# Parallel attention plus product-key experts on one Trainium2 core: two activation blocks moved ahead of the one-hot rows, the last gate stores moved behind loads, attention added into resident totals

## The chip, the core and the metric

The kernel runs on one core of one Trainium2 chip. The metric is device time in microseconds (us) of one execution; three runs of the kernel before are known, and one profiled execution with its trace. In the profile PE is TensorE (PEld its weight loads), DVE is VectorE, ACT is ScalarE, POOL is GpSimd, SP is SyncE, whose queue issues nearly all DMAs. Rows give start and length in us, or a group's busy us and the mean ns of one instruction.

## What is computed

All in float32: 2048 tokens of width 512, 32 heads of width 16, one key and one value head. The second branch has 32 product-key heads, each of which picks 2 of 4096 experts.

```python
x = A_x
xn = _layernorm(x, axis=-1)
return x + _A_ref(xn, A_wq, A_wk, A_wv, A_wo) + _B_ref(xn, B_w_q, B_k1, B_k2, B_u, B_v)

# A: p = softmax(q k^T * Dh**-0.5); out = (p v) @ wo
# B, per token and head: s1, s2 = 64 scores against k1 and k2; the best two of each,
#    the best two of their four sums (top_s, top_e)
g = _softmax(top_s, axis=-1)
ue = u[top_e]; ve = v[top_e]
act = _gelu(jnp.einsum("nd,nhkd->nhk", xf, ue))
out = jnp.einsum("nhk,nhk,nhkd->nd", g, act, ve)
```

## The kernel before

The 2048 tokens are 16 tiles of 128, in four groups of four tiles. Attention needs an exponential for every score, 1024 calls of 128x1024 on ACT, and runs through the whole kernel as 256 steps (`att_steps`, L1040): four pairs of score matmuls (`sc`), four exponentials, sixteen probability-value matmuls (`pv`). Everything else is laid into these steps by hand; no engine's order is left to a scheduler in the main loop (L1147), and every engine runs its queue strictly in the order written.

**The experts** have two ways. Tokens of groups 0 and 1 gather their rows of `u` and `v` by indirect DMA (`gather`, L876); a row is a *slot*: a dot with the token (`dot`, L888), later an add of the weighted row into the tile's total (`add`, L921), both on DVE. Groups 2 and 3 are *dense phases* (`dense`, L648): all 4096 experts are multiplied, in 32 blocks of 128. For a block, 12 matmuls of 128x512 (each product in three split terms, since float32 operands are split into a rounded high half and a rest) give the activations of 512 tokens (`pact`, L799); gelu and the gate rows make `wd`, again as halves; and for each pair of blocks 24 matmuls (`pout`, L783) add into the four totals. The gates of a dense phase come from *one-hot rows*: 32 groups of 16 tokens; for each, DVE compares two index rows with a row of numbers (`onehot`, L721) and 16 small matmuls (`pg`, L752) spread the gates to experts x tokens. ACT copies them to `gst` tiles, which SP stores to `d_g` in DRAM in packets of 256 bytes, two stores of 16 blocks each for every 64 tokens (L760). Each block then reads its 128x512 gate rows back (`fetch_gates`, L669). The `gst` tiles and the `wd` tiles share four buffers; the gate tiles `gy` have three.

**Ahead of a dense phase** the scores of its tokens are made in eight columns c of four tiles each (`item`, L513): 12 matmuls, then 8 maxima and 8 index searches on DVE; after the fourth tile `batch` (L564) makes indices and, through a list that is run two steps later, an exponential and the gates. Then `dense` starts: GpSimd copies the numbers to `io` (L704), the first weights are asked for (`fetch`, L654), three groups of transposes (`ptd`, L714) turn indices and gates into rows.

**What sets the order.** Each step has a `mid` (ACT's and DVE's lists) and a `fill`, in which the score thread (a Python generator) is run until its count of PE time, `spent`, reaches `aim`; at most 4.0 a step are taken. What it yields is a cost; a yield of None ends the step's fill. `store` puts a DMA on a list that SP gets at the start of the next step; `on_act` and `behind` put work on ACT's and DVE's lists of the next `mid`; LAST and LATER hold work for one and two steps on. `dense_on` picks the rate of slots: 1.7 a step outside a phase, 2.5 in its blocks, 1.4 in its one-hot rows; from step 192 of 256 on the rest is spread evenly (L1154).

**The two branches meet** tile by tile. Attention's output for a tile (`block_out`, L423) is either kept: copied to the one `fin` buffer by ACT and stored in `d_part` (L440), to be loaded and added when the experts' total is done (`experts_out`, L446, L452); or, where the experts came first, the stored total is loaded into `fin` and attention's part added to it (L433). Tiles 8 to 11 take the second way, in four steps at the end of the second dense phase's one-hot rows; tiles 0 to 7 the first.

Of the kernel before, what the change touches and what calls it, by code (L numbers as in the profile page):

```python
# [23 lines left out]
P = 128  # L24
# [30 lines left out]
def tile_kernel(ctx, tc, x, wq, wkv, wo, wqT, kT, uv, ub, vb, out):  # L55
# [17 lines left out]
    d_w = [dram.tile([P, KC, 2, 512], F32, name=f"dw{c}") for c in range(NC)]  # L73
    d_g = dram.tile([NB, P, 512], F32, name="dg")
# [164 lines left out]
    def zero_m():  # L239
        z = gtile()  # L240
        nc.gpsimd.memset(z, 0.0)
        nc.sync.dma_start(d_m.rearrange("a h s -> (a h s)").rearrange("(p n) -> p n", p=P), z)

# [140 lines left out]
    DONE_A, DONE_B, OUTS = {}, {}, []  # L384
    WO, lent = [], [0]
# [37 lines left out]
    def block_out(qb, j):  # L423
# [5 lines left out]
        if t in FIN:  # L429
# [14 lines left out]
        DONE_A[t] = True  # L444

    def experts_out(t):  # L446
# [3 lines left out]
        if t in FIN:  # L450
            fin = FIN.pop(t)
            nc.vector.tensor_add(fin, fin, ACC[t])  # L452
            store(lambda: nc.sync.dma_start(out[t * P:(t + 1) * P, :], fin))
        elif t in DONE_A:
# [5 lines left out]
        DONE_B[t] = True  # L460
        return True
# [94 lines left out]
    DT = []  # L556
# [7 lines left out]
    def batch(ph, c, b):  # L564
# [52 lines left out]
        if c == 0:  # L617
            DT.clear()
            dense_tiles()
# [14 lines left out]
        def gates():  # L634
# [8 lines left out]
            stt(dgt[:, :, 1, w], gg, GS, gh, op0=OP.mult, op1=OP.subtract)  # L643

# [3 lines left out]
    def dense(DG, after):  # L648

        df1, df2, dgt = DT[:3]  # L650
# [12 lines left out]
        def gate_tile(b):  # L663
            if b not in gates:
                gy = late[0].tile([P, 2, 512], F32, name="gy", tag="gy", bufs=3)
                gates[b] = gy
            return gates[b]

        def fetch_gates(b):  # L669
            if b < NB and b not in fetched:  # L670
                if formed[0] < b - 2:
# [3 lines left out]
                nc.sync.dma_start(gate_tile(b)[:, 0, :], d_g[b])  # L675
                fetched.add(b)

        splits, halved = {}, set()

        def split(b):  # L680
            if b < NB:
                if b not in raws:
                    run(STORES)
                rw = raws.pop(b)
                us, vs = wk_tile(), wk_tile()
                for i, w in enumerate((us, vs)):
                    nc.scalar.copy(w[:, 0, :], rw[:, i, :])  # L687
                    behind(lambda w=w, i=i: nc.vector.tensor_tensor(out=w[:, 1, :], in0=rw[:, i, :], in1=w[:, 0, :],  # L688
                                                                    op=OP.subtract))
                behind(lambda: halved.add(b))  # L690
                splits[b] = us, vs
# [11 lines left out]
        io = kt(F16, (P, P, TB))  # L703
        nc.gpsimd.tensor_copy(io, iota_h[:, :, None].to_broadcast([P, P, TB]))  # L704
        fetch(0)
        fetch(1)
        yield None
        tr = kt(F16, (P, 3, 512))
        for n, src in enumerate((df1, df2, dgt)):
            if n == 2:  # L710
                yield None
# [550 lines left out]
```

## Time and profile before

| What | Value |
|---|---|
| Runs (device time) | 1992.71, 2001.25, 2004.34 us; median 2001.25 |
| Profiled execution, device time | 2001.03 us |
| Its span, first to last instruction | 1999.3 us |
| Mean granted TensorE clock | 0.967 |
| First dense phase: transposes, one-hot matmuls, blocks | from 607.7, from 618.0, from 753.5 us |
| Second dense phase: the same | from 1451.0, from 1460.4, from 1570.9 us |
| DMA | 494.79 MB, mean 247 GB/s |

A span is a little shorter than the execution's time. The busy shares of all engines are means over stages with different limits, so a stretch is read by itself: in the view by windows each row is a stretch with the busy time and count of each engine, the granted clock of TensorE in it and the share of the DMA engines. In the timeline a bracket tells how long the engine was idle before the group and what released it. The chain of waits follows the work that ended last back from the end. A DMA's row in SP's queue is its issue; in the chain it is issue to landing.

### The profile page before, as it was taken

The numbers are of one execution on the slowest core, as the hardware profiler recorded it, in microseconds if no ns is written. First come the engines' busy times: TensorE is split into PE (matmuls) and PEld (weight loads), VectorE is DVE, ScalarE is ACT, GpSimd is POOL, SyncE is SP. The second block draws the span as 40 slices with busy tenths as digits, with TensorE's granted clock in tenths as the row PEclk, the third lists the DMA queues.
The fourth block names the chain that finished last, engine by engine and source line by source line (L and its number), as shares of the span: only waits on it lengthen the run. The fifth ranks groups of instructions, "written<-read, shape, count | busy, mean of one in ns | idle before, by whom it ended". The sixth has DMA issues, their size and how long they took to land.

```text
span 1999.3 us, 34729 instructions
## 1 busy us (share of the span) xinstructions
PE 1882.9 (94%) x10990; PEld 997.5 (50%) x10990; DVE 1682.7 (84%) x6713; ACT 1292.0 (65%) x1804; POOL 570.8 (29%) x542
## 2 busy tenths in 40 slices
PE   6869999999998998999999999999899789999997
PEld 4534444555554444555555455555445345555552
DVE  7537888999998786999999779999999668999993
ACT  3236666655556785787877565555568567788873
POOL 2202232222222232333444222222223333333320
PEclk9989999999997998999999999999979899999999
DMA  7847878977664878888889877777568877888762
GB/s 272 301 185 235 276 272 272 331 275 248 218 212 140 229 221 271 264 269 269 284 297 328 286 253 261 268 238 225 176 169 234 276 245 263 268 277 257 263 211 63
DMA packets 239882, 494.79 MB, mean 247 GB/s; under 512 B 93380, under 2 KB 93380, under 8 KB 239692
## 3 DMA queue, kind: packets, MB, share of 16 engines
q0 software_dynamic: 73728, 268.47, 40.5%
q1 hardware_dynamic: 163960, 222.44, 34.0%
q10 hardware_dynamic: 2004, 1.61, 0.3%
q8 instruction: 88, 1.44, 0.3%
q14 instruction: 102, 0.84, 0.1%
HBM read 429.51 MB, written 57.64 MB: 244 GB/s over the span
## 4 chain that ended last, share of the span: by engine, by line
PE 63%; DVE 20%; DMA 5%; issue 2%; ACT 2%; SPq 1%; DVEq 0%; ACTq 0%
PE pv L332 18%; PE sc L318 12%; PE psc L532 10%; PE pout L783 8%; PE pact L799 8%; DVE i L547 5%; DVE xa L930 4%; DVE m L545 3%; DVE g L895 3%; PE pg L752 3%; PE pw L487 2%; PE pwo L427 1%; DMA dg<-gst 1%; ACT pt L321 1%; DMA fin<-dpart 1%
## 5 line engine op out<-in xcount | busy, mean ns | idle before, releaser
L321 ACT ACTIVATE pt<-sc 128x1024 f32<-128x1024 f32 x1024 | 993.0, 1025 | 471.1 <-PE sc L318 424.6
L883 POOL DMA_INDIRECT g<-in_uv_dram,idx x512 | 554.0, 1082 | 1358.4 <-DVE xa L930 697.4
L332 PE MATMUL pv<-pt,vaug 128*32 128x512 f32 x4096 | 524.1, 631 | 0.0
L318 PE MATMUL sc<-qa,kaug 64*128 64x512 f32 x2048 | 389.1, 454 | 14.4 <-ACT pt L321 13.5
L532 PE MATMUL psc<-wk,xt 128*128 128x512 f32 x1536 | 388.2, 400 | 5.3 <-DMA xt<-dxt 3.2
L930 DVE SCALAR_TENSOR_TENSOR xa<-g,w,xa 128x512 f32<-128x512 f32 x512 | 370.6, 745 | 0.0
L895 DVE CUSTOM_DVE_ANT_0 g<-g,xa 128x512 f32<-128x512 f32 x512 | 336.1, 681 | 3.0 <-DMA g<-in_uv_dram,idx 3.0
L532 PEld LDWEIGHTS psc<-wk,xt 128*128 128x128 f32 x1536 | 277.8, 188 | 108.7 <-issue 38.5
L318 PEld LDWEIGHTS sc<-qa,kaug 64*128 64x128 f32 x2048 | 157.6, 187 | 338.2 <-ACT pt L321 203.5
L332 PEld LDWEIGHTS pv<-pt,vaug 128*32 128x32 f32 x4096 | 110.7, 113 | 263.4 <-issue 261.7
L799 PE MATMUL pact<-xt,wk 128*128 128x512 f32 x768 | 198.7, 404 | 14.6 <-DVE fin L433 6.3
L547 DVE FIND_INDEX8 i<-m,psc 128x8 uint32<-128x64 f32 x1024 | 206.4, 221 | 0.0
L783 PE MATMUL pout<-wk,wd 128*128 128x512 f32 x768 | 195.7, 402 | 8.7 <-DVE wd L835 4.7
L799 PEld LDWEIGHTS pact<-xt,wk 128*128 128x128 f32 x768 | 141.1, 190 | 65.4 <-issue 17.7
L783 PEld LDWEIGHTS pout<-wk,wd 128*128 128x128 f32 x768 | 140.6, 188 | 56.7 <-DVE wd L835 6.0
L545 DVE MAX8 m<-psc 128x8 f32<-128x64 f32 x1024 | 146.0, 214 | 22.2 <-PE psc L532 19.8
L786 DVE TENSOR_TENSOR da<-da,pout 128x512 f32<-128x512 f32 x128 | 82.7, 679 | 8.2 <-PE pout L783 7.9
L918 DVE SCALAR_TENSOR_TENSOR w<-gth,ga 128x4 f32<-128x4 f32 x128 | 20.2, 158 | 79.9 <-ACT gth L911 79.4
L688 DVE TENSOR_TENSOR wk<-rw,wk 128x512 fp32r<-128x512 f32 x128 | 84.8, 682 | 0.1
L725 DVE TENSOR_TENSOR oh<-oh 128x2048 f16<-128x2048 f16 x64 | 78.0, 1219 | 7.1 <-PE pg L752 7.1
L752 PE MATMUL pg<-oh 128*128 128x32 f16 x1024 | 73.4, 246 | 8.1 <-DVE oh L728 8.1
L687 ACT CAST wk<-rw 128x512 fp32r<-128x512 f32 x128 | 73.6, 628 | 9.0 <-DMA rw<-in_ub_dram 6.7
(150 smaller groups left out, 1341.8 us busy)
## 6 DMA issues: line engine op xcount, KB each, us to landing
wk<-dw SPq DMA_DIRECT2D x96, 512.0 KB
wqt<-in_wqT_dram SPq DMA_DIRECT2D x32, 512.0 KB
dw<-wk SPq DMA_DIRECT2D x32, 512.0 KB
rw<-in_ub_dram SPq DMA_DIRECT2D x64, 256.0 KB
rw<-in_vb_dram SPq DMA_DIRECT2D x64, 256.0 KB
dg<-gst SPq DMA_DIRECT2D x32, 512.0 KB
gy<-dg SPq DMA_DIRECT2D x64, 256.0 KB
qa<-dqh SPq DMA_DIRECT2D x128, 64.0 KB
```

Of the source, the lines that this page charges most:

```text
L318: nc.tensor.matmul(p[:, b, :], kaug[o:o + 64, kc * P:(kc + 1) * P], QA[u][o:o + 64, i, :], start=True, stop=True)
L321: nc.scalar.activation(pt, p, AF.Exp, scale=SCALE)
L332: nc.tensor.matmul(PV[u][32 * j:32 * j + 32, :], vaug[:, kc, :], pt[:, b, :], start=kc == 0, stop=kc == 15)
L532: nc.tensor.matmul(p, XT[g][k][:, a, j * P:(j + 1) * P], WC[n_][k][:, bb, :], start=n == 0, stop=n == 11)
L545: nc.vector.max(m8[:, jb, s, :], p[:, s * E:(s + 1) * E])
L547: nc.vector.max_index(i8[:, jb, s, :], m8[:, jb, s, :], p[:, s * E:(s + 1) * E])
L752: nc.tensor.matmul(p[:, i * NB:(i + 1) * NB], oa[:, :, i], ob[:, :, i], start=True, stop=True)
L783: nc.tensor.matmul(p, wd[:, a, j * P:(j + 1) * P], vs[:, c, :], start=n == 0, stop=n == 5)
L799: nc.tensor.matmul(p, us[:, a, k * P:(k + 1) * P], XT[DG][k][:, c, :], start=n == 0, stop=n == 11)
L883: nc.gpsimd.indirect_dma_start(out=gt, out_offset=None, in_=uv, in_offset=bass.IndirectOffsetOnAxis(ap=IDX[ph, c, ti][:, s:s + 1], axis=0))
L895: nc.vector.tensor_tensor_reduce(u, u, XN[TPH * ph + ti], scale=1.0, scalar=0.0, op0=OP.mult, op1=OP.add, accum_out=a[:, i:i + 1])
L930: nc.vector.scalar_tensor_tensor(acc, v, w[:, i:i + 1], acc, op0=OP.mult, op1=OP.add)
```

## The change

- **Scheduling ahead of a phase.** `dense` is now made before the last score column's tiles. Its first piece, the two weight loads, runs before tile 0; its second, the split of the first halves of blocks 0 and 1, before tile 1; from tile 2 on `dense_on` is 3, where no dots and at most one add a step are issued, until the third transposes are done.
- **Two activation blocks early** (`first`): block 0 before the transposes, block 1 between the first and the second one-hot. Each keeps a copy of its activations in the gate tile and goes through gelu; later it is only scaled by the gate rows.
- **The numbers** `io` are made once at the start, by ACT, stored in DRAM, and loaded in each phase.
- **Splits** of blocks 0, 1 and 2 come at rows 24, 27 and 31 instead of 30 and 31; the three right-hand one-hot tiles become one (`obs`).
- **The last gate stores** are cut into blocks 0 to 2, 3 to 15 and 16 to 31; the first goes at once, with the gate rows of these three blocks behind it; the second goes out with block 2, ahead of the totals' loads; the third after block 3.
- **Blocks**: the output sums start one block later; the product of blocks 3 and 4 with the gates goes to DVE's list.
- **Totals in place**: a tile whose total is resident (`LIVE`, tiles 0 to 7) gets attention's part added there by DVE, and its total is stored straight to the output.

```diff
+    LIVE = set(range(GT))
...
-        if t in FIN:
+        if t in LIVE:
+            acc = ACC[t]
+            behind(lambda: nc.vector.tensor_add(acc, acc, p))
+        elif t in FIN:
...
-        DONE_A[t] = True
+        DONE_A[t] = t in LIVE
...
+        elif DONE_A.get(t):
+            acc = ACC[t]
+            store(lambda: nc.sync.dma_start(out[t * P:(t + 1) * P, :], acc))
...
+            if c == NC - 1:
+                gated_all.append(True)
...
         def fetch_gates(b):
             if b < NB and b not in fetched:
-                if formed[0] < b - 2:
+                if (b == 3 and multiplied[0] < 2) or (b > 3 and formed[0] < b - 2):
...
-        io = kt(F16, (P, P, TB))
-        nc.gpsimd.tensor_copy(io, iota_h[:, :, None].to_broadcast([P, P, TB]))
+
         fetch(0)
         fetch(1)
-        yield None
+        yield 0.0
+        early = []
+        on_act(lambda: early.extend(half_split(b, 0) for b in range(2)))
+        yield 0.0
+        df1, df2, dgt = DT[:3]
...
+        def first(b):
+            p = xtile("pact")
+            for k in activations(b, early[b], p):
+                if k < KC - 1:
+                    yield 3 * UNIT
+            g, y = gate_rows(b), hh[:, b, :]
+            nc.scalar.activation(y, p, AF.Square, scale=C_CUB ** 0.5)
+            nc.scalar.copy(g, p)
+            nc.vector.scalar_tensor_tensor(y, y, C_IN, p, op0=OP.add, op1=OP.mult)
+
+            def go():
+                nc.scalar.activation(y, y, AF.Tanh)
+                behind(lambda: nc.vector.scalar_tensor_tensor(y, y, 1.0, g, op0=OP.add, op1=OP.mult))
+
+            LATER.append(go)
+            yield 3 * UNIT
...
+        io = kt(F16, (P, P, TB))
+        nc.sync.dma_start(io, d_io)
...
+        yield from first(0)
+        for n in range(2):
+            spread(n)
             yield 0.45
+        while not gated_all:
+            yield None
+        spread(2)
...
+        obs = kt(F16, (P, 3, NB, TB))
         onehot(0)
+        yield from first(1)
         onehot(1)
...
-                    if t0 == 448:
-                        store(first_gates)
+                    if t0 < 448:
+                        store(lambda: (part(0, 16), part(16, NB)))
+                    else:
+                        store(lambda: (part(0, 3), first_gates()))
+                        rest_of_gates.extend([lambda: part(3, 16), lambda: part(16, NB)])
...
-                later_split(q - NQ + 2)
+            if q in (NQ - 8, NQ - 5, NQ - 1):
+                later_split((NQ - 8, NQ - 5, NQ - 1).index(q))
...
+                        if b == 2:
+
+                            store(lambda: (rest_of_gates.pop(0)(), load_totals()))
...
+            def scaled(y=y, g=g):
+                multiplied[0] += 1
+                stt(y, g, 1.0 / GS, y, op0=OP.mult, op1=OP.mult)
...
+                if b in (3, 4):
+
+                    behind(lambda gated=gated, g=g, p=p: gated(g, p))
+                else:
+                    gated(g, p)
                 behind(whole)
-            yield 3 * UNIT
-            if b == 0:
-                yield None
+            if b == 3:
+                store(lambda: rest_of_gates.pop(0)())
+                later_split(4)
...
+            dn = None
+            if ph >= NSP and c == NC - 1:
+                dn = dense(ph, n + 1 if n + 1 < len(SEQ) else None)
+                yield next(dn)
             for ti in range(TPH):
+                if dn and ti == 1:
+                    yield next(dn)
+                if dn and ti == 2:
+                    dense_on[0] = 3
...
-                pos += 2.1 if len(IDX) < NC * TPH else (1.7, 2.5, 1.4)[dense_on[0]]
+                pos += 2.1 if len(IDX) < NC * TPH else (1.7, 2.5, 1.4, 0.0)[dense_on[0]]
             else:
-                pos += max(0.0, NSL - pos) / max(half - 4 - d, 1)
+                pos += max(0.0, NSL - pos) / max(half - 4 - d, 1) if dense_on[0] < 3 else 0.0
...
+                if dense_on[0] == 3:
+                    sums = min(sums, 1)
...
         ACC[t], XN[t] = xa[:, 0, :], xa[:, 1, :]
+        LIVE.add(t)
```

More of the change, by code (lines that the diff above doesn't have):

```diff
@@ L460, in experts_out @@
         DONE_B[t] = True
+        LIVE.discard(t)
         return True
@@ L683, in split @@
                     run(STORES)
[L684 to L689, printed above, removed]
+                us = half_split(b, 0) if b > 1 else None
+                splits[b] = us, half_split(b, 1)
                 behind(lambda: halved.add(b))
-                splits[b] = us, vs
+                raws.pop(b)
         def later_split(b):
@@ L812, in dense @@
[L812 to L818 removed]
+            wd = []
+            if b > 1:
+                if b not in halved:
+                    yield None
+                if b not in halved:
+                    flush()
+                p = xtile("pact")
+                for k in activations(b, splits[b][0], p):
+                    if k == 0:
+                        store(lambda b=b: fetch_gates(b + 1))
+                        if b % 2 == 0 and b not in (2, 4):
+                            later_split(b + 2)
+                        if b == 2:
+                            store(lambda: (rest_of_gates.pop(0)(), load_totals()))
+                    if k == KC - 1 and b == NB - 1 and after is not None:
+                        wp_read(after, range(2))
+                    if b == NB - 1 and after is not None:
+                        load_phase2_xt(SEQ[after][0], k)
+                    if k < KC - 1:
+                        yield 3 * UNIT
+                if b not in fetched:
+                    if b > 3 and formed[0] < b - 2:
+                        flush()
+                    run(STORES)
+                    assert b in fetched
```

126 lines of the change are left out of this document (62 added, 64 removed).

## The prediction

> **What bounds the kernel now.** First I read the page: span, busy shares, the 40 slices.
>
> ```profile
> span 1999.3 us, 34729 instructions
> PE 1882.9 (94%) x10990; PEld 997.5 (50%) x10990; DVE 1682.7 (84%) x6713; ACT 1292.0 (65%) x1804; POOL 570.8 (29%) x542
> ...
> PE   6869999999998998999999999999899789999997
> ...
> PEclk9989999999997998999999999999979899999999
> ```
>
> TensorE sets the pace; its idle digits and its dips of the granted clock sit together, at slices 13 to 16 and 29 to 33. These are the two dense phases' beginnings, which the change rewrites. Only what is idle or slowly clocked there can be won. The view by windows cuts the two places into stretches (length, then busy time and count of PE, PEld, DVE, ACT, POOL, clock, DMA share, GB/s):
>
> ```profile
> 600.00:625.00 25.00, 17.49 (x116) 7.37 (x114) 23.43 (x107) 14.95 (x23) 7.49 (x6) 0.83 0.44 138
> 740.00:755.00 15.00, 12.53 (x67) 4.43 (x66) 11.24 (x32) 11.14 (x16) 7.76 (x8) 0.77 0.90 284
> 755.00:790.00 35.00, 25.38 (x124) 13.05 (x123) 22.47 (x51) 20.51 (x31) 8.35 (x8) 0.85 0.80 268
> 1440.00:1465.00 25.00, 13.43 (x96) 7.00 (x92) 24.32 (x121) 10.57 (x16) 4.24 (x4) 0.75 0.35 122
> 1465.00:1550.00 85.00, 84.65 (x764) 43.84 (x756) 79.23 (x166) 69.12 (x117) 24.69 (x21) 0.87 0.80 212
> 1550.00:1565.00 15.00, 12.40 (x104) 6.12 (x102) 14.79 (x38) 11.30 (x22) 4.49 (x4) 0.89 0.87 231
> 1585.00:1645.00 60.00, 46.36 (x216) 20.64 (x214) 38.10 (x89) 31.23 (x43) 19.93 (x17) 0.86 0.76 262
> ```
>
> PE's idle time (length less busy) is 7.5, 2.5, 9.6, 11.6, 0.4, 2.6 and 13.6 us, 48 in all. The timeline of PE names what ended the largest gaps (start, length, group, then in brackets the idle time before it and its releaser), and the chain of waits names the transfers behind them:
>
> ```profile
> 607.69 1.09 PE L714 MATMUL ptd<-ident,da 128*128 128x128 f32 x8 [0.72 <-DVE da L631]
> 618.02 1.19 PE L752 MATMUL pg<-oh 128*128 128x32 f16 x16 [2.68 <-DVE oh L728]
> 753.53 3.01 PE L799 MATMUL pact<-xt,wk 128*128 128x512 f32 x12
> 773.77 1.22 PE L799 MATMUL pact<-xt,wk 128*128 128x512 f32 x2 [4.98 <-ACT wk L687]
> 778.24 2.07 PE L799 MATMUL pact<-xt,wk 128*128 128x512 f32 x4 [3.25 <-DVE wk L688]
> 1451.04 1.97 PE L714 MATMUL ptd<-ident,da 128*128 128x128 f32 x8 [8.69 <-DVE da L631]
> 1591.81 2.93 PE L799 MATMUL pact<-xt,wk 128*128 128x512 f32 x6 [6.34 <-DVE fin L433]
> 1638.97 1.84 PE L783 MATMUL pout<-wk,wd 128*128 128x512 f32 x6 [3.60 <-DVE fin L433]
> ```
>
> ```profile
> 745.58 14.97 DMA dg<-gst
> 763.78 11.24 DMA rw<-in_vb_dram
> ...
> 1568.58 13.71 DMA dg<-gst
> 1585.77 5.20 DMA fin<-dpart
> 1595.15 7.33 DMA out_dram<-fin
> 1602.55 5.66 DMA fin<-dpart
> ```
>
> So there are two kinds of hole. At a phase's start PE has run out of score matmuls while DVE still works through arg-maxima, dots and adds, and the one-hot rows come late. At the end of the one-hot rows SP's queue holds the last two gate stores, and behind them, in program order, the gate rows, the totals, block 3's weights and, in the second phase, attention's partial (fin), whose wait stops DVE and then PE.
>
> **The change part by part.** *Start of a phase* (holes 7.5 and 11.6). Two activation blocks of 12 matmuls go ahead: 3.01 us each by the row at 753.53. Block 0 lies before the transposes, block 1 between the first and second one-hot. The work is the same, but done where PE waited. DVE skips dots, and keeps at most one add a step, over the last two score tiles, and gets two weight halves to subtract early:
>
> ```profile
> L895 DVE CUSTOM_DVE_ANT_0 g<-g,xa 128x512 f32<-128x512 f32 x512 | 336.1, 681 | 3.0 <-DMA g<-in_uv_dram,idx 3.0
> L895 DVE DVE_READ_ACCUMULATOR2_ANT act<- 128x1 f32 x512 | 41.2, 80 | 0.0
> L930 DVE SCALAR_TENSOR_TENSOR xa<-g,w,xa 128x512 f32<-128x512 f32 x512 | 370.6, 745 | 0.0
> L688 DVE TENSOR_TENSOR wk<-rw,wk 128x512 fp32r<-128x512 f32 x128 | 84.8, 682 | 0.1
> L725 DVE TENSOR_TENSOR oh<-oh 128x2048 f16<-128x2048 f16 x64 | 78.0, 1219 | 7.1 <-PE pg L752 7.1
> ```
>
> Ahead of the indices stand some two dots (0.68 + 0.08) and two adds, 2.9 us, against two subtractions, 1.4 us: DVE comes 1.5 us earlier. In the second phase it also loses a stall: one small gate instruction ran 2.53 us beside GpSimd's copy of the number rows, and a like one later 0.18:
>
> ```profile
> 1435.74 2.53 DVE L641 TENSOR_SCALAR gh<-gd 128x32 f16<-128x32 f32 x1
> 1436.33 1.90 POOL L704 COPY oh<-iota_h 128x2048 f16<-128x2048 f16 x1
> 1457.60 0.18 DVE L641 TENSOR_SCALAR gh<-gd 128x32 f16<-128x32 f32 x1
> ```
>
> That copy becomes a load from DRAM. The Trainium skill (SBUF — State Buffer, "SBUF: two separate sides") says DVE in a two-port mode and GpSimd take their shared port pair as an exclusive lock; the two overlapping rows agree. Block 0's 3.0 and DVE's 1.5 + 2.3 leave 1.8 of the 8.69; block 1's 3.0 covers the 2.7 wait for the first one-hot. What is late next is the gates' exponential, queued two steps behind the indices: the third transposes stay behind it, 1 to 2 us. I take 5 us off the first start, 9 off the second (bounds: 7.5 and 11.6 won, or 6 lost each should ACT wait for the early halves, below).
>
> *End of the one-hot rows* (holes 2.5 + 9.6 and 13.6). Weights for blocks 2 and 3 are asked for at rows 24 and 27 of 32, three to four steps before the last gate stores, so the waits at 773 and 778 go. SP's new order is: gate rows' store of blocks 0 to 2 (3 of 32 blocks), their loads, block 4's weights, the store of blocks 3 to 15, four loads of totals, block 3's gate load, then the last store. Bytes stay the same. DVE now waits for gate rows in three places: block 2's product at once, and the scaling of blocks 0 and 1. Behind them on DVE stand dots, adds and the weights whose tanh ACT waits for ahead of four exponentials, then PE. The store and its load are a round trip: in the chain two full stores take 14.97, the fin loads 5.20 and 5.66. I estimate 8 to 9 us from the step's start to landing, against 5 to 8 at which DVE asks: 3 us lost a phase (bounds 0 and 8). So 9.6 less 3, and 2.5 us for slow clock after the gap (four matmuls in 2.07 at 778 against 1.0 by the row at 753.53): 9 in the first phase. The 2.5 at 740 stays: there ACT's exponentials limit an empty step.
>
> In the second phase attention's block outputs fall into the same steps. With both blocks moved ahead, the one-hot rows end about two steps later against them, so the first partial's load no longer stands behind 13.71 us of stores; the single fin buffer still makes each later load wait for the output's store (7.33 + 5.66). I take 8 of 13.6 away and 3 us of slow clock: 11 (bounds 0 and 16).
>
> *What it costs.* Skipped dots and adds come back. Three steps a phase at 1.7 slots, and fewer steps at the rate of 2.5, are about 12 slots of 0.68 + 0.08 + 0.745 = 1.5 us: 18 us of DVE. From step 192 the planner spreads them over 60 steps, 0.3 us each, where DVE is at 90% and PE full; there they lie beside PE. But two more pairs of one-hot rows fall behind step 192, where DVE limits already (14.79 of 15 busy in 1550 to 1565): 4 us lost (bounds 0 and 10), and 2 more for the rest. At the start one ACT copy of 128x2048 (twice the 1025 ns of the 128x1024 exponential: 2 us, bounds 0 and 4) and a 512 KB store lie where PE already waits; I take 1.
>
> *Totals in place*, and ACT's time for a copy:
>
> ```profile
> L321 ACT ACTIVATE pt<-sc 128x1024 f32<-128x1024 f32 x1024 | 993.0, 1025 | 471.1 <-PE sc L318 424.6
> ...
> L440 ACT COPY fin<-pwo 128x512 f32<-128x512 f32 x8 | 4.8, 595 | 0.3 <-DMA dpart<-fin 0.3
> L452 DVE TENSOR_TENSOR fin<-fin,xa 128x512 f32<-128x512 f32 x8 | 5.5, 684 | 5.3 <-DMA fin<-dpart 5.3
> L433 DVE TENSOR_TENSOR fin<-fin,pwo 128x512 f32<-128x512 f32 x4 | 2.7, 685 | 25.3 <-DMA fin<-dpart 25.3
> ```
>
> Tiles 0 to 7 lose 8 ACT copies, 8 stores and 8 loads; their 8 DVE adds only move. ACT has room and L452's wait falls in the tail, beside attention: I cost this at nothing (bounds -3 and +3: each add now holds its accumulator until DVE comes, while one-hot products use the other two). The costly line, L433, is for tiles 8 to 11 and stays.
>
> *Sum*: -5 -9 -9 -11 +4 +2 +1 +0 = -27; the two copies into gate tiles (4 of 0.59 us on ACT) and late buffers I put at +3. So 2001.03 (the profiled execution; its span is 1999.3) - 24 = 1977. The median of the runs, 2001.25, is 0.2 away, so nothing is shifted.
>
> **The rivals.** *SP's waits only change places*: gate rows and partials come as late as the weights did, the ends win nothing of their 9 and 11: 1977 + 20 = 1997. For it: the same bytes, one queue, DMA share 0.80 and 0.90. Against: the load asked for earliest was the one that stopped PE.
>
> *DVE's debt*: all 18 us of skipped work on the path instead of 2: 1993. For it: 14.79 of 15. Against: the later dense blocks, where PE is full.
>
> *Early halves late*: ACT's two early casts wait for weights asked for one score tile (5 us) before, and a load took 11.24 under load; 6 us twice: 1989. Against: DMA share 0.35 there.
>
> *Clock*: slow steps follow idle time alone.
>
> ```profile
> 622.25 3.64 PE L332 MATMUL pv<-pt,vaug 128*32 128x512 f32 x16
> ...
> 657.86 1.92 PE L332 MATMUL pv<-pt,vaug 128*32 128x512 f32 x16
> ...
> 1497.86 3.13 PE L332 MATMUL pv<-pt,vaug 128*32 128x512 f32 x16
> ```
>
> In the one-hot rows some steps run pv at 3.1 to 3.6 instead of 1.9 us: the first row above, the last, and seven between them, each 1.2 to 1.7 us too long, 13 us together. Were the gaps at the phases' starts their cause, they would go too: 1964. Against it: the window 1465 to 1550 has a clock of 0.87 with PE busy 84.65 of 85. The Trainium skill (TensorE: Matmul & The Clock Gate, Part 1) states this rule, half clock after an idle window of about 3.4 us; the trace agrees after the 8.69 us gap and not inside the stage.
>
> *The slower one: held buffers.* The last gate rows' tiles share four buffers with the blocks' products (wd). Their two stores now go out a step apart and after loads, so blocks 2 and 3's casts on ACT wait for them with four exponentials queued behind. The stores go out some 10 us before the cast. As long as they land within that, nothing happens; at 15 (14.97 in the chain) each of four casts loses 5 us, 1997; if the totals' loads push it to 19.5, 9.5 each, 38 us: 2015. It decides from 18.5 us on. For it: the DMAs move 268 and 262 GB/s around the stores, against 122 at the second start. Against: half a store each, and the first gates' stores absorbed 15 us before.
>
> **How the numbers follow.** Forecast 0.53 (own range 1962 to 1990), waits change places 0.11, debt 0.09, late halves 0.07, clock 0.10, held buffers 0.10. The range 1955 to 2000 reaches past the clock case by half its gain and over the first three rivals; it leaves out the slower one and some of each tail. Runs before spread from 1992.71 to 2004.34, and 0.5% (10 us) is about what a measurement of this kernel can tell from no change. Faster by more, below 1991: forecast, clock and late halves, 0.70, and about a tenth of the 0.20 at 1993 to 1997, 0.02: 0.72. Slower: held buffers and 0.01: 0.11. Within: 0.17.
>
> **What would show it.** Right: 12 pact matmuls ahead of ptd and of the first pg; no gap there above 3 us; no ACT wait for rw at the first blocks; L433's wait well below 25.3; L440 and L452 gone; no POOL copy in a phase. Wrong: DVE waiting for gy more than 3 us a phase, ACT waiting for gst's stores, or PE idle above 2 us in every one-hot step after step 192.

## The result: slower, 2011.7 us against 1998.9

The changed kernel took 2011.7 us in the median of 8 runs (1999.98 to 2014.78), the kernel before 1998.85 of 8 runs on the same chip: ratio 1.0056, 95% interval 1.0029 to 1.0084. The profiled execution took 2011.38 us (before: 2001.03). Its page has nearly the same busy time and holes a little elsewhere:

```profile
span 2009.7 us, 34697 instructions
...
PE 1885.2 (94%) x10990; PEld 1001.6 (50%) x10990; DVE 1681.6 (84%) x6713; ACT 1292.8 (64%) x1801; POOL 563.2 (28%) x540
...
PE   6869999999999997999999999999999859999997
...
PEclk9989999999998898999999999999998979999998
```

TensorE is busy 2.3 us longer and the span is 10.4 us longer, so 8.1 us are idle time. The kernels do the same attention in the same order, so the copy at the end of each attention unit (`e<-pv`, one of 32) marks the same place in both. The view by windows, cut at these copies, gives the start of the first phase, its end, the start of the second and its end; before:

```profile
551.54:665.20 113.66, 106.15 (x730) 54.50 (x730) 106.03 (x496) 72.36 (x106) 26.16 (x24) 0.89 0.58 178
765.74:838.82 73.08, 63.46 (x336) 35.22 (x336) 59.77 (x131) 49.10 (x73) 23.26 (x20) 0.93 0.76 249
1400.91:1467.37 66.46, 54.89 (x328) 29.56 (x330) 63.52 (x363) 34.41 (x44) 15.11 (x14) 0.90 0.46 157
1567.23:1701.08 133.85, 119.16 (x607) 58.45 (x609) 96.05 (x227) 85.98 (x121) 46.30 (x42) 0.94 0.80 266
```

and after:

```profile
551.85:666.72 114.87, 109.20 (x738) 57.71 (x740) 101.30 (x480) 75.68 (x109) 19.45 (x18) 0.91 0.54 155
766.96:841.30 74.34, 63.84 (x329) 35.88 (x331) 58.89 (x132) 48.40 (x71) 22.96 (x20) 0.91 0.78 248
1402.87:1464.38 61.51, 57.56 (x336) 31.92 (x338) 55.14 (x342) 36.95 (x48) 11.59 (x12) 0.97 0.51 165
1565.80:1709.70 143.90, 112.92 (x613) 56.23 (x615) 100.12 (x239) 85.01 (x122) 48.87 (x45) 0.89 0.82 260
```

Length less TensorE's busy time is its idle time: 7.5, 9.6, 11.6 and 14.7 us before, 5.7, 10.5, 3.9 and 31.0 after. The starts gained 9.5 us, the ends lost 17.2. The starts in the timeline of PE: the blocks' matmuls stand where the plan put them, and the 8.69 us wait at the second transposes is 2.63.

```profile
601.89 3.02 PE L736 MATMUL pact<-xt,wk 128*128 128x512 f32 x12
608.84 1.11 PE L761 MATMUL ptd<-ident,da 128*128 128x128 f32 x4 [3.93 <-DVE da L644]
...
1442.27 0.98 PE L736 MATMUL pact<-xt,wk 128*128 128x512 f32 x3 [1.15 <-DVE w L1000]
...
1451.32 1.83 PE L761 MATMUL ptd<-ident,da 128*128 128x128 f32 x8 [2.63 <-DVE da L644]
...
1460.57 1.23 PE L817 MATMUL pg<-oh 128*128 128x32 f16 x16
```

At the ends TensorE now stops inside blocks 3 and 4, for the second (rest) halves of their weights, and once for ScalarE's exponentials:

```profile
761.82 2.56 PE L736 MATMUL pact<-xt,wk 128*128 128x512 f32 x10 [0.91 <-DVE wk L701]
...
772.94 4.63 PE L736 MATMUL pact<-xt,wk 128*128 128x512 f32 x10 [4.00 <-DVE wk L701]
...
788.00 4.63 PE L736 MATMUL pact<-xt,wk 128*128 128x512 f32 x10 [4.82 <-DVE wk L701]
...
1615.80 3.92 PE L736 MATMUL pact<-xt,wk 128*128 128x512 f32 x10 [14.23 <-DVE wk L701]
...
1643.50 1.71 PE L322 MATMUL sc<-qa,kaug 64*128 64x512 f32 x4 [13.79 <-ACT pt L325]
```

A stop also slows what follows it: ten matmuls took 2.56 us behind a gap of 0.91, and 4.63 behind 4.00 and 4.82. The Trainium skill (TensorE: Matmul & The Clock Gate, Part 1) says the clock falls to half after an idle window of about 3.4 us; the first three rows agree. The fourth, 3.92 us behind a gap of 14.23, is slowed by less.

What stands behind 14.23 is read from the timeline of DVE, that behind 13.79 from the rows of ACT and SP:

```profile
1603.59 0.69 DVE L977 CUSTOM_DVE_ANT_0 g<-g,xa 128x512 f32<-128x512 f32 x1 [4.32 <-DMA g<-in_uv_dram,idx]
...
1606.40 0.69 DVE L977 CUSTOM_DVE_ANT_0 g<-g,xa 128x512 f32<-128x512 f32 x1 [2.11 <-DMA g<-in_uv_dram,idx]
...
1613.79 0.69 DVE L441 TENSOR_TENSOR fin<-fin,pwo 128x512 f32<-128x512 f32 x1 [5.96 <-DMA fin<-dpart]
...
1615.06 0.69 DVE L701 TENSOR_TENSOR wk<-rw,wk 128x512 fp32r<-128x512 f32 x1
```

```profile
1628.98 0.62 ACT L907 CAST wd<-gy 128x512 fp32r<-128x512 f32 x1
1641.91 0.62 ACT L907 CAST wd<-gy 128x512 fp32r<-128x512 f32 x1 [12.30 <-DMA dg<-gst]
```

```profile
1619.56 0.43 SPq L442 DMA_DIRECT2D out_dram<-fin  x1
1625.64 0.33 SPq L425 DMA_DIRECT2D fin<-dpart  x1
1627.87 0.32 SPq L693 DMA_DIRECT2D gy<-dg  x1
1632.83 0.34 SPq L442 DMA_DIRECT2D out_dram<-fin  x1
1633.22 0.43 SPq L825 DMA_DIRECT2D dg<-gst  x1
```

VectorE waits for gathered rows, then 5.96 us for a finished row block, and only then subtracts the weight half that TensorE needs. ScalarE reached a product's cast at 1629.6, but the store that holds that memory left only at 1633.22, behind three waits in SP's queue, and took 8.61 us to land, by the chain of waits:

```profile
1633.22 8.61 DMA dg<-gst
```

That is the rival "held buffers", with one cast instead of four.

### The profile page after: what moved, and what is told of

The parts are those of the page before. It is cut to its first block, busy times and chain, and to the rows that moved or that the text cites. A ratio compares the mean times of both kernels' runs of the same rounds, so it can differ in the third digit from the quotient of the medians.

```text
span 2009.7 us, 34697 instructions
## 1 busy us (share of the span) xinstructions
PE 1885.2 (94%) x10990; PEld 1001.6 (50%) x10990; DVE 1681.6 (84%) x6713; ACT 1292.8 (64%) x1801; POOL 563.2 (28%) x540
## 4 chain that ended last, share of the span: by engine, by line
PE 61%; DVE 19%; DMA 5%; issue 4%; ACT 2%; POOL 1%; SPq 0%; ACTq 0%; DVEq 0%; POOLq 0%
PE pv L336 17%; PE sc L322 12%; PE psc L544 9%; PE pout L853 9%; PE pact L736 9%; DVE i L559 5%; DVE m L557 3%; DVE xa L1012 3%; DVE g L977 3%; PE pg L817 2%; PE pwo L432 1%; ACT pt L325 1%; PE pw L499 1%; DMA out_dram<-fin 1%; POOL g L965 1%
## 5 line engine op out<-in xcount | busy, mean ns | idle before, releaser
L336 PE MATMUL pv<-pt,vaug 128*32 128x512 f32 x4096 | 518.7, 625 | 0.0
L977 DVE CUSTOM_DVE_ANT_0 g<-g,xa 128x512 f32<-128x512 f32 x512 | 335.9, 682 | 15.6 <-DMA g<-in_uv_dram,idx 15.6
L817 PEld LDWEIGHTS <-oh 128*128 128x128 f16 x1024 | 68.6, 163 | 14.4 <-issue 8.9
```

What stands on the lines that cost most here:

```text
L336: nc.tensor.matmul(PV[u][32 * j:32 * j + 32, :], vaug[:, kc, :], pt[:, b, :], start=kc == 0, stop=kc == 15)
L817: nc.tensor.matmul(p[:, i * NB:(i + 1) * NB], oa[:, :, i], ob[:, :, i], start=True, stop=True)
L977: nc.vector.tensor_tensor_reduce(u, u, XN[TPH * ph + ti], scale=1.0, scalar=0.0, op0=OP.mult, op1=OP.add, accum_out=a[:, i:i + 1])
```

## The experiments

Theory at the outset: the starts win as forecast, and the second end loses it to the held buffer (A) and to VectorE's queue (B), in the form of late gathers (B1) or of the order of its work (B2). Ratios are to the kernel before on the same chip. Idle is TensorE's idle time in the whole first phase (attention units 8 to 12) and the whole second (23 to 27), from the windows, in the profiled execution. Where intervals of two runs overlap, as those of neighbours here mostly do, the time alone doesn't tell them apart; then the trace does or nothing does.

| Run | Median us | Ratio, 95% interval | Idle us |
|---|---|---|---|
| before | 1998.85 | 1 | 19.8, 29.2 |
| after | 2011.7 | 1.0056, 1.0029 to 1.0084 | 19.4, 39.0 |
| e1 stores at once | 2004.0 | 1.0026, 1.0006 to 1.0046 | 23.4, 29.8 |
| e2 no hold of dots | 2019.5 | 1.0114, 1.0084 to 1.0143 | 26.1, 39.0 |
| e3 ring of 11 | 2015.1 | 1.0081, 1.0053 to 1.0109 | 19.6, 40.8 |
| e4 ring of 11, two totals buffers | 2013.3 | 1.0082, 1.0053 to 1.0110 | 20.8, 44.9 |
| e5 stores at once, totals last | 1997.2 | 0.9989, 0.9963 to 1.0015 | 24.5, 24.7 |
| e6 no totals in place | 2011.5 | 1.0058, 1.0037 to 1.0079 | 19.9, 39.8 |
| e7 product behind | 2008.0 | 1.0045, 1.0027 to 1.0062 | 20.3, 36.8 |
| e8 before, totals last | 1988.6 | 0.9947, 0.9924 to 0.9970 | 16.0, 24.8 |
| e9 e5, subtractions first | 1997.5 | 0.9988, 0.9962 to 1.0013 | 20.7, 19.4 |
| e10 e5, halves a step earlier | 1996.2 | 0.9969, 0.9947 to 0.9992 | 19.9, 29.3 |
| e11 e8, subtractions first | 2001.0 | 0.9979, 0.9958 to 1.0000 | 18.9, 25.6 |
| e12 e9 and e10 | 1998.1 | 0.9982, 0.9958 to 1.0007 | 22.6, 21.5 |
| e13 e5, one block early | 1990.4 | 0.9957, 0.9929 to 0.9984 | 17.4, 19.7 |
| e14 after, no round trip | 2001.5 | 1.0005, 0.9980 to 1.0031 | 19.4, 33.8 |
| e15 before, no round trip | 1998.6 | 1.0007, 0.9979 to 1.0036 | 21.1, 31.0 |
| e16 e5, no round trip | 1991.2 | 0.9963, 0.9941 to 0.9984 | 21.2, 20.1 |
| e17 e10, no round trip | 1980.8 | 0.9905, 0.9873 to 0.9937 | 18.2, 18.9 |
| e18 e13, two totals, ring of 11 | 1998.8 | 0.9983, 0.9962 to 1.0004 | 17.9, 20.9 |

**e1: the stores at once.**

```diff
-                        store(lambda: (part(0, 3), first_gates()))
-                        rest_of_gates.extend([lambda: part(3, 16), lambda: part(16, NB)])
+                        store(lambda: (part(0, 3), first_gates(), part(3, 16), part(16, NB)))
```

> The changed kernel with the last two gate stores issued right behind the gate loads of blocks 0 to 2, no longer in two pieces at blocks 2 and 3. Theory A (held buffers: the last store leaves only at 1633.2 us behind SP's chain through the one totals buffer, it holds the staging tile whose memory the next weight tile takes, ScalarE's cast waits 12.3 us for it): that wait goes, the 13.8 us stop of TensorE at 1643 shrinks below 3 us, and the time falls by 8 to 12 us, to 2000 to 2004. Theory B (the loss is VectorE's, whose sums come late because gathers do): the stop only moves to the next wait for VectorE, and the time falls by at most 3 us, 2009 or more; it may rise by up to 5, since 928 KB leave in front of the raw weight rows of blocks 2 and 3.

2004.0 us: A's size. The stop of 13.8 is gone; the waits of PE in 1420 to 1720 us say what is left (total, times, longest):

```profile
PE pact L736 <- DVE wk L701: 17.2, 1, 17.2
...
PE sc L322 <- ACT pt L325: 3.0, 4, 1.4
```

The trace shows the held buffer; in time the intervals of the two kernels still overlap. It was one of two stops; the other grew from 14.2 to 17.2, since the totals addition ahead of the subtraction now waited 10.86 us.

**e2: no hold.** The two lines that set `dense_on` to 3 are left out.

> The changed kernel without the mark that holds back new dots during the last two gate items ahead of each dense phase. Theory B (the sums held back at the second start are caught up in the second end, 18 dots between 1580 and 1600 us where the kernel before had 9, so that the ring of gathers runs empty and VectorE stands 9 us for gathers at 1590 to 1608): the 14.2 us stop of TensorE at 1615.8 shrinks below 6 us, the starts lose 3 to 8 us again (a wait of the transposes for VectorE's totals of 5 us or more a phase comes back), and the time comes out between 2003 and 2010. Theory A (held buffers alone): both stops at the second end stay within 3 us of their size, and the time rises by 3 to 8 us, to 2015 to 2020.

2019.5 us, as A had it: both stops stay (11.7 and 12.3) although VectorE's waits for gathers fell from 15.6 to 5.6 us; the totals addition waits in their place. So the hold earns its keep, and late gathers (B1) weren't what bound.

**e3 and e4: two totals buffers.** `NGB = 12` becomes 11; in e4 `fin` also gets `bufs=2`.

> The changed kernel with a ring of 11 gather tiles in place of 12: the control of the next run, which needs the 4 KB per partition. Theory A: within 4 us of the changed kernel (2008 to 2016), both stops at the second end still there. Theory B: the ring runs empty sooner, VectorE's wait for gathers grows from 15.6 us to 20 or more, and the time rises by 4 to 12 us.

> The changed kernel with 11 gather tiles and two totals buffers in place of one, so that the load of a finished row block doesn't wait until the block before it has landed in DRAM. To be read against the run with 11 gather tiles alone. Theory A: SP's wait of 10.9 us in front of a totals load at 1598 goes, the last gate stores leave 10 us earlier or more, ScalarE's 12.3 us wait shrinks below 4, and the time is 8 to 16 us below that of 11 gather tiles alone. Theory B: the late gathers keep VectorE where it is, and the time is at most 4 us below it.

The two are the same (1.0081 and 1.0082), so A's account of SP's chain was wrong in one point. With two buffers the totals load left at once, but the last store left no sooner: in program order it stands behind a gate load and an output store that wait for VectorE (e4):

```profile
1621.32 0.43 SPq L425 DMA_DIRECT2D fin<-dpart  x1
1629.54 0.32 SPq L693 DMA_DIRECT2D gy<-dg  x1
1632.94 0.34 SPq L442 DMA_DIRECT2D out_dram<-fin  x1
1633.33 0.43 SPq L825 DMA_DIRECT2D dg<-gst  x1
```

e3 confirms B's wait (25.8 us for gathers), though its time can't be told from that of the changed kernel.

**e5: totals last.** On top of e1, additions into finished row blocks go behind the rest of the step's list.

```diff
-            behind(total)
+            TOTALS.append(total)
...
-                rest = BEHIND[:]
+                rest = BEHIND + TOTALS
```

> The kernel with all gate stores sent at once, and on VectorE the additions into the finished row blocks (fin) put behind the weight subtractions of the same step instead of ahead of them. To be read against the run with the stores at once alone (ratio 1.0026, where TensorE still stood 17.2 us at block 3 for the subtraction, which itself stood 10.9 us behind an addition that waited for its row block from DRAM). Theory B2 (VectorE's order: the wait for DRAM stands in front of the subtraction): that stop falls to 8 us or less, and the time to 1994 to 1999. Theory B1 (late gathers and late weight rows would stop the subtraction anyway): the stop stays above 12 us and the time within 3 us of 2004.

1997.2 us, and the stop is 5.1: B2. In the timeline of DVE the subtraction comes 12.6 us ahead of the addition it stood behind:

```profile
1608.56 0.68 DVE L701 TENSOR_TENSOR wk<-rw,wk 128x512 fp32r<-128x512 f32 x1
...
1621.18 0.69 DVE L441 TENSOR_TENSOR fin<-fin,pwo 128x512 f32<-128x512 f32 x1 [8.80 <-DMA fin<-dpart]
```

With e1 and e5 the second end's two long stops are accounted for, and e5 is the first run here whose interval lies clear below the changed kernel's. The late addition itself now makes TensorE wait 4.8 us. e5 has the new starts and still is only level with the kernel before.

**e6: no totals in place.** `LIVE` stays empty.

> The changed kernel without attention's part added into totals in place: ScalarE copies the part and SP stores it and loads it back, as in the kernel before. All theories put the loss elsewhere: within 4 us of the changed kernel, 2008 to 2016, with both stops of the second end in place. If the in-place addition is what costs (it adds to VectorE in the one-hot rows and lets the ring run late), the time falls by 5 us or more and the wait for gathers at the second end below 8 us.

2011.5 us, both stops in place (10.8 and 13.8): this part of the change costs and wins nothing.

**e7: block 2's product behind.** `if b in (3, 4)` becomes `if b in (2, 3, 4)`.

> The changed kernel with the product of block 2 with its gate rows also put behind the step's other work on VectorE, as those of blocks 3 and 4 are, so that the round trip of the gate rows through DRAM doesn't stand in front of the dots and the weight subtractions. Theory C (at the first end VectorE waits 2.0 us for the gate rows with the subtraction of block 3 behind it, and TensorE stands 4.0 us): the stops of TensorE at the first end for that subtraction fall from 9.7 us to under 6, and the time by 2 to 5 us, to 2007 to 2010. Rival: block 3's subtraction stays late since its cast and its raw rows come only one step ahead; the stops stay within 2 us, and the time within 2 us of 2011.7.

The stops of the first end are 11.1 us, not below 6: C fell. The time, 2008.0, can't be told from 2011.7.

**e8: the kernel before with totals last.**

> The kernel before with only that order changed: additions into finished row blocks behind the weight subtractions. In the kernel before VectorE waits 25.3 us at these additions, and TensorE 6.3, 3.6 and 1.4 us at the second end behind them. If the order is what costs there, the three waits fall by 5 us or more in sum, and the time by 4 to 9 us, to a ratio of 0.9955 to 0.998. If something else comes last (raw rows of weights, the gate rows), the time stays within 3 us.

The lowest ratio of any run that leaves nothing out: 0.9947, though the three waits only fell from 11.3 to 7.8. Its profiled execution took 1976.57 us, the shortest of its twelve, so its places aren't to be taken one by one; and e11, which has this order and one edit more, came out at 0.9979, so the size of the gain is uncertain. It is the fair neighbour of e5, which has the same order. The ratio falls here by 0.0053 and from e1 to e5 by 0.0037: the order is a fault of both kernels, and it explains the stop but not the difference between them. The second phases of e8 and e5 have the same idle time (24.8 and 24.7). In the first phase e5 has 8.5 us more, and at the first end 16.0 us against 4.1. That end is looked at next.

**e9 to e12: the first end by order and by lead.** e9 runs the subtractions ahead of the dots; e10 moves `later_split(4)` to the beginning of block 2 and splits blocks 2 and 3 at rows 29 and 31; e11 is e9's edit on e8; e12 is e9 and e10.

> The kernel of the stores at once and totals last (1997.2 us, ratio 0.9989), and the weight subtractions of blocks 2 and later put ahead of the dots of their step on VectorE. There TensorE stood 15.4 us at the first end for these subtractions, and 5.4 at the second. Theory B2 (VectorE's order: dots and sums stand in front of them): both sums of stops are halved or better, 8 and 3 us or less, and the time falls by 5 to 10 us, to 1987 to 1992. Rival D (the halves are only made in the step in which TensorE wants them, and VectorE must wait for ScalarE's cast of the same step wherever it stands): the stops shrink by less than a third, VectorE's wait for that cast grows, and the time stays within 3 us of 1997.

> The same kernel of the stores at once and totals last, with the order on VectorE left alone, but the halves of blocks 3 and 4 made a step earlier: those of blocks 2 and 3 at the third-last and the last one-hot step, those of block 4 at the beginning of block 2. Rival D: the stops of TensorE at the first end fall from 15.4 to under 6 us, those at the second end don't grow, and the time falls by 6 to 11 us, to 1986 to 1991. Theory B2: the subtraction is still behind dots and sums that wait, and the raw rows of the weights aren't there a step earlier (ScalarE waits for them 2 us or more): the stops stay above 10 us and the time within 3 us of 1997.

> The kernel before with totals last (ratio 0.9947, 1988.6 us), and the weight subtractions ahead of the dots. In its profile TensorE waits 1.4 us for these subtractions at the first end and none at the second, where 7.8 us are left at one totals addition. All theories: small, within 4 us of 1988.6. It is faster by more only if the subtractions also stand behind what makes that addition late.

> Both edits at once on the kernel of the stores at once and totals last: halves of blocks 3 and 4 a step earlier, and subtractions ahead of the dots. If either edit alone takes the stops away, this one adds nothing to the better of the two (within 3 us). If the order and the lead each hold part of the stops, it is 3 us or more below the better one, 1982 to 1987, and the stops of TensorE for the halves fall under 3 us at both ends.

The stops named did go, from 15.4 us to 1.3 in e9, to 5.0 in e10, to nothing in e12. The idle time at the first end didn't: 16.0 in e5, then 13.4, 12.6 and 15.4. In the waits of PE in 580 to 850 us others stand in their place, in e9

```profile
PE pout L854 <- DVE wd L912: 6.8, 1, 6.8
PE sc L322 <- ACT pt L325: 5.7, 9, 2.8
```

and in e12

```profile
PE sc L322 <- ACT pt L325: 15.6, 8, 13.2
```

Neither order nor lead alone sets the first end. e11's edit won nothing either: 0.9979 against 0.9947, intervals that overlap.

**e13: one block left at the end.** A new theory (E): the two blocks' matmuls had been the cover of what comes late behind the one-hot rows, gate rows above all. Block 1 goes back behind them:

```diff
-        yield from first(1)
...
-            if b > 1:
+            if b > 0:
                 if b not in halved:
```

> The kernel of the stores at once and totals last (1997.2 us), with only block 0's activations ahead of the one-hot rows; those of block 1 stay at the end of the phase as in the kernel before. Theory E (the two blocks' matmuls covered the round trip of the last gate rows through DRAM at the end; moved to the start they leave it bare): idle time of TensorE at the first end falls from 16.0 to 11 us or less, the starts give back at most 3 us each, and the time is 1990 to 1995. Rival: the chain at the end is set by products and halves whatever TensorE has to do, so the first end keeps its idle time, the starts lose, and the time is 1997 to 2004.

1990.4 us, in the range that E gave (0.9957 against 0.9989, but with intervals that overlap). The whole first phase in the windows, e5 and then e13 (the same 1797 matmuls in each):

```profile
555.27:840.33 285.06, 260.58 (x1797) 136.88 (x1799) 231.72 (x768) 200.31 (x296) 72.19 (x64) 0.94 0.68 203
```

```profile
556.61:841.22 284.61, 267.22 (x1797) 137.03 (x1799) 234.37 (x773) 200.16 (x296) 74.37 (x65) 0.93 0.69 207
```

Idle time falls from 24.5 to 17.4 us, at the first end from 16.0 to 4.3 (2.9 of it comes back in the one-hot rows). This is more than the spread between profiles: at the first end the fourteen profiles with both blocks moved have 9.3 to 16.0 us, e13 and e18 with one block moved have 4.3 and 5.6, and the four with none moved (before, e8, e11, e15) have 4.1 to 9.6. With the one-hot rows counted in, it is 12.7 to 18.8, then 10.0 and 10.5, then 7.0 to 12.3. A lower granted clock took the first phase's gain back in this execution (267.22 us busy against 260.58), whose time was 1996.7.

**e14 to e17: without the round trip.** `d_g[b]` in `fetch_gates` becomes `vb[b]`: the stores are made, but the gate rows come from an input and no load waits for the stores. These four leave the stored gates out of the result. e14 is the changed kernel with that, e15 the kernel before, e16 e5, e17 e10.

> The changed kernel with the gate rows of the dense blocks loaded from an input of the same size (the rows of the second weight) in place of the stored one-hot products: the stores are still made, but no load waits for them, so the output isn't the reference's. Theory E: TensorE's idle time at the first end falls from 10.5 to 5 us or less, and at the second end by 4 us or more (the held staging tile is still there); the time falls by 8 to 12 us, to 2000 to 2004. Rival: the idle time at the first end stays above 8 us and the time within 4 us of 2011.7.

> The kernel before with the same replacement of the gate rows by an input (the output isn't the reference's either). Theory E: two blocks' matmuls cover the round trip there, so that little is won: within 4 us of the kernel before, a ratio of 0.998 to 1.001. If it falls by as much as the changed kernel does (8 us or more), the round trip costs both kernels the same and theory E falls.

> The kernel of the stores at once and totals last (1997.2 us) with the gate rows loaded from an input (output not the reference's). Theory E: idle time of TensorE at the first end falls from 16.0 to 8 us or less and at the second from 14.0 to 10 or less; the time falls by 8 to 13 us, to 1984 to 1989. Rival: within 4 us of 1997.

> The kernel of the stores at once and totals last with the halves of blocks 3 and 4 a step earlier and the gate rows loaded from an input (output not the reference's). If late halves and the round trip together are what the moved matmuls covered, TensorE's idle time at the first end falls to 6 us or less (16.0 without either edit, 12.6 and 13.0 with one), and the time to 1980 to 1987. If it stays at 9 us or more, something else in the chain of a block (Square, Tanh and product between ScalarE and VectorE) sets the pace of the first end, and the time is 1988 to 1993.

In time E holds: without the round trip the changed kernel is 10 us faster (1.0056 to 1.0005, intervals that just touch) and the kernel before not at all (1.0007). For e5 the difference, 0.9989 to 0.9963, lies within the intervals; for e10, 0.9969 to 0.9905, it is clear. So, as far as the time tells, the round trip is covered before and bare after. In place E was partly wrong. The first end and the second in e14:

```profile
762.73:835.56 72.83, 63.52 (x329) 35.66 (x331) 57.73 (x129) 48.46 (x71) 22.95 (x20) 0.91 0.78 240
1564.41:1703.11 138.70, 115.32 (x613) 56.91 (x615) 100.41 (x239) 85.28 (x123) 48.77 (x45) 0.90 0.83 269
```

The idle time that goes lies at the second end (31.0 to 23.4, in e16 14.0 to 9.5), while the first end keeps 9.3 and in e16 13.0. For the first end e17's time suggests that halves and gate rows together matter (ratio 0.9905, where each alone gave 0.9969 and 0.9963); its profile doesn't show it, since that execution took 1995.18 us, the longest of six (four took 1977.1 to 1981.3), with 11.4 us idle at the first end. What of the first end is due to which stays open. No run puts both blocks back and keeps the rest of the change, and none takes the round trip out of e13.

**e18: two totals buffers on e13.**

> The kernel with one block's activations early, stores at once and totals last (1990.4 us, ratio 0.9957), with two totals buffers and, to pay for them, 11 gather tiles. If the single buffer is what makes the last totals addition late, TensorE's 8.8 us stop there falls below 4 and the time to 1983 to 1988. If the row block is late for the queue and the rings anyway, as two buffers were worth nothing in the changed kernel, the stop stays above 6 us, VectorE's wait for gathers grows, and the time is 1990 to 1996.

TensorE's stop for the last totals addition fell from 8.8 to 3.8 as hoped, but the ring of 11 took more: 7.2 us idle between the phases against 3.5, and 1998.8 us.

## Why the prediction was wrong, step by step

- *First start, -5*: idle time went from 7.5 to 5.7, in the other runs with both blocks and the hold to 5.5 to 6.0. Right in kind, 2 instead of 5. *Second start, -9*: 11.6 to 3.9. Right, 7.7 of 9; DVE is late next, by 2.63, where the working had 1.8. The small gate instruction that ran 2.53 us beside GpSimd's copy takes 0.18 now that the copy is gone.
- *"The work is the same, but done where PE waited."* This step failed. The 24 matmuls (two groups of 3.01 us) also stood between the last gate stores and the first work that needs them, and no price was put on taking that cover away. That the round trip costs the changed kernel about 10 us and the kernel before nothing is seen in time (e14, e15); that one block left at the end is worth at least 2 to 4 us of idle time at the first end is seen in the profiles (e13, e18 against the fourteen). What that block covers there is more than the round trip, since e14 and e16 keep their idle time at the first end.
- *First end, -9*: the waits at 773 and 778 went, and stops of 4.00 and 4.82 for the next blocks' halves came at once. "What is late next" was asked for the gate rows and not for the halves of blocks 3 and 4, which are made in the step that uses them. The term was also measured on one execution: e8, whose program is the same up to the second end, had 4.1 us idle there instead of 9.6.
- *Second end, -11*: came out as +16.3 of idle time. This step failed too. VectorE's wait for fin did fall, from 25.3 to 6.0, but TensorE won nothing by it. The working saw the row block come earlier, but not that gathers, the addition and the weight subtraction stand in one queue in this order (14.23 us, e5), nor that a cast would wait for the last gate store (13.79 us, e1).
- *Held buffers*, the rival with 0.10: the mechanism is shown by e1. Its point of decision was wrong. It isn't the landing time, 8.61 us and far below 18.5; "the stores go out some 10 us before the cast" failed, the last one left 3.6 us after ScalarE was ready.
- *Totals in place, 0*: right (e6). *The startup, +1*: idle time up to unit 7 is 49.8 before and 49.6 after, nothing. *DVE's debt*: not the cause (e2).
- *Early halves late*: not seen; the early blocks' matmuls waited at most 1.15 us, and ScalarE waited for no weights at either start. *Clock*: the gaps at the starts shrank by 9.5 us, and the granted clock in 1465 to 1550 us was 0.87 before and 0.88 after.
- *The signs it named*: of those for wrong, ScalarE waiting for the gate stores came (12.30 us). Of those for right, no gap above 3 us at the starts failed once, by 3.93 us at 608.84.
- *SP's waits only change places*, 1997: nearest in kind, but the ends lost more than they had to win.

The forecast of 1977 is 35 us too low. Idle time at the second end makes 24 of it (+16.3 where 8 were taken off), that at the first end 7.5 (+0.9 where 6.6 were taken off), the starts 4.5 (-9.5 where 14 were taken off). The 5.5 us hoped for from a faster clock at the two ends didn't come either, and TensorE was busy 2.3 us longer. That is some 44 us; against it stand the 10 us of costs in the sum, of which nothing shows as idle time outside these four places (+0.4).

## What to carry to other kernels

Before work is moved out of a late stage into a hole, ask what that work was covering where it stood, and put a price on that: here half of the move (one block of two) kept part of the cover, and TensorE's idle time in the two phases fell from 49.2 us in e5 to 37.1 in e13 (49.0 in the kernel before). In an engine's hand-written queue, what waits for DRAM belongs behind what the busiest engine waits for; that one reordering made the kernel before faster (0.9947), and the changed kernel needs it, the early stores and half the move to come as far (0.9957). So no run with a right result shows that the change wins anything over the reordering alone. A stop that is removed shows only which stop is next; idle time of the whole phase says more, and it takes more than one execution.

## What the runs showed of the hardware that was not expected

The same order of instructions differs by several microseconds between executions, in the DMA queue and in the clock. Up to the second end e8's program is that of the kernel before; SP's issue of the last two gate stores, in the kernel before and in e8:

```profile
745.58 10.97 SPq L760 DMA_DIRECT2D dg<-gst  x2
```

```profile
741.84 5.60 SPq L760 DMA_DIRECT2D dg<-gst  x2
```

The weights behind them in the queue follow at 763.31 in the one and at 756.84 in the other. The first phase took 287.3 and 274.5 us, again the kernel before and e8:

```profile
551.54:838.82 287.28, 267.45 (x1794) 136.47 (x1796) 240.61 (x796) 201.32 (x301) 81.77 (x73) 0.92 0.72 218
```

```profile
551.48:826.00 274.52, 258.49 (x1794) 135.48 (x1796) 239.92 (x796) 201.42 (x301) 83.01 (x73) 0.96 0.75 228
```

Of these 12.8 us only 3.8 are idle time; 9.0 are TensorE's busy time for the same 1794 matmuls, at a granted clock of 0.92 and 0.96. Over all twenty profiles this busy time is 258.5 to 272.7 us in the first phase and 261.2 to 274.9 in the second, but 277.8 to 278.5 from the second phase's end to the last copy, where the clock is 1.00. So inside a phase TensorE's busy time differs by up to 14 us from profile to profile, as much as the stops that the experiments remove. The clock differs without any gap, too. In 625 to 665 us the changed kernel and e1 have the same program, and TensorE was busy 39.70 of 40 us in both, at 0.85 and 0.91:

```profile
625.00:665.00 40.00, 39.70 (x350) 20.58 (x352) 36.53 (x77) 32.67 (x54) 7.05 (x5) 0.85 0.55 134
```

```profile
625.00:665.00 40.00, 39.70 (x371) 20.97 (x370) 38.03 (x80) 34.16 (x58) 7.05 (x5) 0.91 0.56 140
```

No run here tells what sets it.
